# State update in 64 by 64 tiles, last step's stores, and a new order of work in a gated recurrence with a maxout layer

## The chip, the cores and the metric

The kernel runs on one core of one Trainium2 chip. The core has five engines with a queue each: TensorE (PE in the profile, its weight loads PEld), VectorE (DVE), ScalarE (ACT), GpSimd (POOL) and SyncE (SP), which here only issues DMA transfers. The metric is device time in microseconds (us), the median of several runs; lower is better.

## What is computed

Two stages follow each other. The first is a recurrence for 4 batches of 8 heads over 768 tokens, with a state of 48 by 48 per head; the second is a layer that takes the maximum of three products and projects it back.

```python
for t in range(S):
    state = alpha[:, :, t, :, None] * state + np.einsum('bhd,bhe->bhde', k[:, :, t], v[:, :, t])
    y[:, :, t] = np.einsum('bhd,bhde->bhe', q[:, :, t], state)
...
h = np.maximum(np.maximum(x @ w1, x @ w2), x @ w3)
return (h @ w_out).astype(np.float32)
```

x is y with its 8 heads side by side: 3072 tokens of 384 numbers. w1 to w3 are 384 by 768, w_out is 768 by 384.

## The kernel before

The 3072 tokens are worked in 12 steps of 256 tokens (two tiles of 128). Step s belongs to batch s mod 4, so each batch has three steps. In a step the recurrence is turned into matrix products: the logarithms of alpha are summed (`sums`), q and k are scaled by the exponentials of the sums (`scaled`), turned so that the feature dimension lies on the partitions (`turn`, or by a DMA transpose in `turn_by_dma`), multiplied to scores (`scores`), masked (`masked`), and applied to v together with the state left by the earlier tokens (`attend`). `update`, `add_state` and `decay_state` carry the state on. The layer follows: `gate` has nine products a step, `maxed` takes the maximum, `project` multiplies by w_out, `store` scales a tile of 128 tokens and writes it out.

The order of all instructions is written by hand, in three strings: PROLOGUE (the first steps, and the loads of the weights), STEADY (once for each s from 3 to 10) and LAST (s = 11). `emit` reads them piece by piece. A piece is a letter, an index, perhaps a letter for the engine or the memory bank, and the step relative to s after the @: `S0@1` is the state update of step s+1. Each engine executes its own instructions in the order in which the pieces stand, and so does SP with its transfers. The letters:

- l: load of a step (0 alpha, 1 k, 2 q, 3 v); K: load of a weight block (0 to 8 for w1 to w3, 9 to 11 for w_out); W: its cast to fp16
- H: warm matmuls, as many as the index says, on a blank tile; their result is not used
- m, N, r: product of alpha in pairs, logarithms, inverse; u, w: k and q of the first token of a pair; c: sums; e, f, g: their exponentials; k, q: scaling; V: scaling of v
- T, t: turning on TensorE and the copy out of PSUM; D: turning by DMA (from step 5 on); A: scores of one half of the heads; a: mask
- Y: attend; x: its copy; M, S, s, z: gates, update, sum and decay of the state
- G, h: the nine gate products and maxima; O, o: projection and store of one tile

An engine letter is v (VectorE), p (POOL) or a (ACT); without one a default holds: k, q, u, w, m, M, z and W go to POOL, t and s to VectorE, V, x, o and the first h of three to ACT. N, r, e, f and g always run on ACT, the masks and the other h always on VectorE. A letter g behind T, c, A, Y or O (or s) names the PSUM banks; there are four banks g, two s and two w, taken in turn, and a piece that takes a bank waits until the one that had it is read.

The state update (`update`) writes one PSUM tile per tile of tokens x. It contracts over 64 token pairs, so x = 0 lies on partitions 0 to 63 and x = 1 on 64 to 127. The two heads of a pair are 128 columns of weights. In the last four steps, the last of their batch, only x = 0 is updated. The scores (`scores`) use rows of one head (48 of 64) and 64 columns, so four matmuls have tiles of their own.

All loads and stores are issued by SP but the two small constants, which ACT issues at the start. Loads have four buffers per input; a load waits until its buffer has been used.

Of the kernel before, what the change touches and what calls it, by code (L numbers as in the profile page):

```python
# [23 lines left out]
def kernel(  # L24
# [12 lines left out]
    nc = tc.nc  # L37

    B, H, S, D = q.shape
    NT, DM = out.shape  # L40
    DF = moe_w_out.shape[0]
    P = 128
# [3 lines left out]
    U = 2  # L46
    R = 2
# [4 lines left out]
    HP = H // 2  # L52
# [77 lines left out]
    vs_c, ys_c, half_c = c32[:, 0:1], c32[:, 1:2], c32[:, 2:4]  # L130
# [23 lines left out]
    def times(eng, dst, src, col):  # L154
        if eng == "a":
            nc.scalar.mul(dst, src, col)  # L156
        else:
            engines[eng].tensor_scalar_mul(dst, src, col)
# [14 lines left out]
    def bank(shape, name, tag, dtype=FP32):  # L173
        return ps.tile(shape, dtype, name=name, tag=tag, bufs=banks[tag])
# [184 lines left out]
    def update(s, _, tag):  # L359
        qk, vt = qks[s % NQ], vts[s % NQ]  # L360
        xs = range(U) if s + B < NS else range(1)
        for x in xs:
            sps_of[s, x] = bank([P, HP, 2, D], "sps", tag or "s")
        for p in range(HP):
            for r in range(R):
                for x in xs:
                    rows = slice(x * J, (x + 1) * J)
                    nc.tensor.matmul(sps_of[s, x][:, p],  # L368
                                     qk[rows, r, 1, p].rearrange("p a b -> p (a b)"),
                                     vt[rows, r * HP + p, :, :D], start=(r == 0), stop=(r == R - 1))  # L370

    def add_state(s, x, eng):
        c, b = divmod(s, B)
# [48 lines left out]

    def store(s, x, eng):
        c, b = divmod(s, B)
        ob = work.tile([P, DM], FP32, name="ob", tag="ob", bufs=5)
        times(eng or "a", ob, ops_of.pop((s, x)), ys_c)
        row = b * S + (U * c + x) * P
        nc.sync.dma_start(out[row:row + P, :], ob)

    def warm(_, n, *x):  # L430
        wps = bank([P, 512], "wps", "g")
# [8 lines left out]
        "k": scale_k, "q": scale_q, "V": values,  # L440
        "T": turn, "t": keep_turned, "D": turn_by_dma, "A": scores, "a": masked,
        "Y": attend, "x": keep_x, "M": gates, "S": update, "s": add_state, "z": decay_state,
        "G": gate, "h": maxed, "O": project, "o": store,
    }

# [9 lines left out]
    def emit(s, order):  # L455
# [5 lines left out]
                pieces[piece[0]](step, i, eng)  # L461

    PROLOGUE = """
        H7@0 l0@1 l0@2 H4@0 m0p@0 N0@0 H4@0 r0@0 r1@0 H3@0 H1@0 w0p@0
        c0@0 u0v@0 f0@0 H2@0 e0@0 m0p@1 q1v@0 H4@0 V0@0 H6@0 k1v@0 g0@0
        r0@1 N0@1 k0v@0 l2@1 l1@1 l3@1 r1@1 T1@0 q0v@0 l2@2 M0p@0 H3@0
        m0v@2 l1@2 T0g@0 c0g@1 H3@0 N0@2 r0@2 l3@2 t0@0 K2@0 e0@1 g0@1
        S0@0 f0@1 t1@0 K0@0 k1v@1 u0v@1 s0a@0 A0g@0 r1@2 A1g@0 V0@1 l0@3
        c0@2 q1v@1 H5@0 w0p@1 f0@2 a1@0 a2@0 e0@2 k0p@1 g0@2 q0p@1 a3@0
        H4@0 K1@0 T1@1 H2@0 l0@4 M0p@1 t1a@1 z0v@0 s1@0 T0@1 a0@0 K6@0  # L470
        S0@1 u0v@2 Y0g@0 q1p@2 M0p@2 t0a@1 K3@0 w0p@2 s0a@1 k1v@2 V0@2 A1@1
        K7@0 H7@0 K4@0 a3@1 x1@0 a2@1 k0v@2 x0@0 q0p@2 A0g@1 K8@0 z0p@1
        T1@2 a1@1 T0@2 t1a@2 a0@1 Y0g@1 K5@0 t0a@2 W1p@0 A1@2 s1a@1 A0g@2
        W2a@0 W0v@0 S0@2 m0p@3 x1@1 x0v@1 G0@0 s0a@2 G0@1 a2@2 a0@2 a1@2
        l2@3 a3@2 N0@3 r0@4 m0p@4 G1@0 h0@0 l1@3 c0@3 G1@1 r1@4 l3@3
        e0@3 h0v@1 h1@0 W3p@0 G2@1 W6a@0 r0@3 h1@1 f0@3 G2@0 h2@1 G6@0
        z0p@2 h2@0 h6@0 G3@0 W4v@0 h3@0 Y0g@2 K9@0 G4@0 W7p@0 N0@4 r1@3
        x0v@2 c0@4 h4@0 W8p@0 x1@2 G7@0 W5a@0 h7@0 G3@1 h3v@1 K11@0 g0@4
        e0@4 g0@3 w0v@3 G6@1 G8@0 M1p@0 K10@0 h6v@1 G5@0 k1p@3 l2@4 G4@1
        G0@2 l1@4 l3@4 q1p@3 h8@0 h5@0 V0@3 u0p@3 h4@1 G5@1 q0v@3 h5@1  # L480
        G7@1 s1a@2 h0@2 k0p@3 W9a@0 G6@2 f0@4 G8@1 T1@3 h7@1 T0@3 t1a@3
        l1@6 h8@1 W11p@0 h6@2 G1@2 t0@3 l0@5 S0@3 W10p@0 h1@2 A1@3 A0g@3
        z1p@0 k1p@4 a1@3 a0@3 a2@3 a3@3 M0p@3 G3@2 O0g@1 w0v@4 G7@2 s0a@3
        z0p@3 l2@5 o0v@1 O1@0 m0p@5 O0g@0 h7@2 q1v@4 l1@5 s1@3 o1v@0 h3@2
        l3@5 O1g@1 l0@7 r0@5 o1@1 l0@6 G2@2 o0v@0 G4@2 h2@2 l3@6 q0p@4
        h4@2 Y0g@3 l1@7 u0v@4 G8@2 x0v@3 k0p@4 V0@4 l2@6 l3@7 l2@7 x1v@3
        G5@2 h5@2 h8@2 r1@5
    """
    STEADY = """
        T1g@1 u0p@2 T0@1 G0@0 t1@1 N0@2 w0p@2 t0a@1 c0@2 g0@2 h0v@0 f0@2  # L490
        G3@0 q0v@2 G4@0 e0@2 G5@0 G1@0 M1v@-2 h3@0 k1v@2 h4@0 h5@0 z1p@-2
        h1@0 M0p@1 S0@1 q1p@2 k0p@2 D1@2 A0g@1 A1@1 a0@1 V0@2 s0@1 a2@1
        z0p@1 a1@1 G6@0 a3@1 D0@2 s1@1 O1g@-1 O0@-1 h6@0 o1@-1 o0@-1 G7@0
        Y0g@1 G2@0 h7@0 h2@0 r0@3 G8@0 r1@3 x0@1 m0p@3 h8@0 x1@1 l1@5
        l2@5 l0@5 l3@5
    """
    LAST = """
        G0@0 G1@0 G3@0 G6@0 h0@0 G2@0 h1@0 G4@0 h3@0 G7@0 h6@0 G8@0
        h4@0 O1@-1 h2@0 G5@0 h7@0 O0@-1 o1@-1 h8@0 h5@0 o0@-1 O1g@0 O0@0
        o1v@0 o0@0  # L500
    """

    blank = cpool.tile([P, 512], FP16, name="blank")
# [36 lines left out]
```

## Time and profile before

| | |
|---|---|
| median of 5 runs | 155.5 us (155.26 to 156.53) |
| profiled execution | 155.5 us; its span from first to last instruction 153.7 us |
| granted TensorE clock, mean | 0.995 |
| first gate matmul starts | 26.57 us |
| first matmul of STEADY starts | 53.68 us |
| last matmul group starts | 147.04 us |
| matmuls, weight loads | 2539 each |
| bytes moved | 32.50 MB, mean 211 GB/s |

How to read the profile: each engine has a row of its busy time; a group of instructions is named by its line, its engine, and what it writes and reads (gps are the gate products, ops the projection, sps the state update, aps the scores, yps attend, tps the turning, lps the sums, wps the warm matmuls; qk holds scaled q and k, qkT the turned ones, lat the masked scores). Busy time is not time on the path; what sets the end is read from the chain of waits, which goes back from the last instruction to what released it, and from the order of time. The slices by time:

```profile
PE   6997998999999999999999999999999999999990
DVE  2188959979999999699699699696895995784460
DMA  5999999999992899999999999999818047011023
```

Transfers are dense until slice 28 of 40. The steps of STEADY follow each other from about 54 to 139 us, 10.67 us apart.

### The profile page before, as it was taken

Reading aid. Unit: us, or ns where it says so; the run is one execution under the profiler, and the core shown is the slowest. Engines: PE = TensorE matmul, PEld = TensorE weight load, DVE = VectorE, ACT = ScalarE, POOL = GpSimd, SP = SyncE. Lnnn points to the kernel's source line nnn. Section 1 sums busy time; section 2 is a strip of 40 time slices with the busy share of each in tenths; the row PEclk is TensorE's granted clock in tenths of the full one; section 3 lists DMA queues with packets and bytes.
Section 4 is the critical chain, followed back from the end, with each engine's and each line's share of the span. In section 5 each row is a group of like instructions: output and inputs, shape, how many; then the busy total and the mean of one; then the engine's idle time right before and its main releaser. Section 6 shows DMA issues by size and latency. Waiting matters only on the chain.

```text
span 153.7 us, 5939 instructions
## 1 busy us (share of the span) xinstructions
PE 146.8 (96%) x2539; PEld 109.7 (71%) x2539; DVE 119.1 (77%) x214; ACT 82.7 (54%) x164; POOL 82.7 (54%) x112
## 2 busy tenths in 40 slices
PE   6997998999999999999999999999999999999990
PEld 2454656878976797786786886877867877868860
DVE  2188959979999999699699699696895995784460
ACT  3379568984460573753755646646727633143331
POOL 5365977618964259839549469289197280020000
PEclk9999999999999999999999999999999999999998
DMA  5999999999992899999999999999818047011023
GB/s 132 321 325 324 348 335 350 324 256 316 306 289 74 209 339 289 260 142 337 226 198 285 207 271 233 160 294 280 212 40 206 3 63 184 3 51 55 0 75 134
DMA packets 72890, 32.50 MB, mean 211 GB/s; under 512 B 65440, under 2 KB 72864, under 8 KB 72864
## 3 DMA queue, kind: packets, MB, share of 16 engines
q1 hardware_dynamic: 72576, 31.99, 82.5%
q8 instruction: 20, 0.33, 0.9%
q10 hardware_dynamic: 288, 0.13, 0.5%
q14 instruction: 6, 0.05, 0.1%
HBM read 23.73 MB, written 4.72 MB: 185 GB/s over the span
## 4 chain that ended last, share of the span: by engine, by line
PE 77%; DVE 7%; DMA 6%; issue 3%; POOL 2%; ACT 1%; DVEq 0%; POOLq 0%
PE gps L396 36%; PE ops L420 14%; PE wps L433 9%; DMA qkT<-qk 6%; PE yps L330 5%; PE aps L280 4%; PE yps L311 3%; PE sps L368 2%; PE tps L259 2%; DVE hT L411 1%; DVE lat L287 1%; POOL qa L203 1%; DVE qkT L152 1%; DVE qa L203 1%; PE lps L209 1%
## 5 line engine op out<-in xcount | busy, mean ns | idle before, releaser
L396 PE MATMUL gps<-xT,wcat 128*128 128x256 f16 x648 | 77.9, 273 | 0.1
L396 PEld LDWEIGHTS <-wcat 128*128 128x128 f16 x648 | 60.9, 98 | 10.0 <-issue 0.2
L383 POOL TENSOR_TENSOR st<-full,gm 128x384 f16<-128x384 f32 x19 | 17.4, 914 | 31.8 <-DVE gm L355 21.4
L411 DVE TENSOR_TENSOR hT<-gps,h 128x512 f16<-128x512 f32 x36 | 24.2, 689 | 11.9 <-PE gps L396 10.7
L287 DVE TENSOR_TENSOR lat<-aps,cp 128x512 f16<-128x512 f32 x48 | 30.5, 680 | 2.0 <-PE aps L280 1.9
L150 ACT CAST h<-gps 128x512 f16<-128x512 f32 x25 | 14.8, 591 | 27.9 <-PE gps L396 21.9
L411 DVE TENSOR_TENSOR h<-gps,h 128x512 f16<-128x512 f32 x36 | 24.5, 683 | 5.7 <-PE gps L396 3.7
L420 PE MATMUL ops<-wo,hT 128*128 128x384 f16 x144 | 25.4, 326 | 0.0
L156 ACT ACTIVATE ob<-ops,c 128x384 f32<-128x384 f32 x20 | 11.6, 581 | 15.2 <-PE ops L420 15.2
L420 PEld LDWEIGHTS <-hT 128*128 128x128 f16 x144 | 14.1, 98 | 8.0
L433 PE MATMUL wps<-blank 128*128 128x512 f16 x55 | 15.1, 426 | 2.2 <-DVE blank L505 1.2
L184 POOL TENSOR_TENSOR pa<-ra 128x384 f32<-128x384 f32 x11 | 11.1, 1015 | 3.8 <-DMA ra<-in_alpha_dram 3.8
L235 POOL TENSOR_TENSOR qk<-ka,ic 128x384 f16<-128x384 f32 x10 | 10.2, 1018 | 5.4 <-DVE ka L199 4.0
L150 ACT CAST xT<-yps 128x384 f16<-128x384 f32 x20 | 8.7, 483 | 5.7 <-PE yps L330 5.7
L433 PEld LDWEIGHTS <-blank 128*128 128x128 f16 x55 | 5.5, 107 | 8.8 <-issue 3.8
L156 ACT ACTIVATE vt<-rv,c 128x768 f16<-128x768 f32 x12 | 11.5, 956 | 0.5 <-DMA rv<-in_v_dram 0.4
L330 PE MATMUL yps<-lat,vt 64*32 64x128 f16 x768 | 11.1, 220 | 0.5 <-issue 0.2
L203 POOL TENSOR_TENSOR qa<-rq,ra 128x384 f32<-128x384 f32 x10 | 10.0, 1001 | 2.8 <-ACT ra L195 2.3
L330 PEld LDWEIGHTS <-vt 64*32 64x32 f16 x768 | 7.3, 90 | 3.0 <-issue 0.4
L150 ACT COPY qkT<-tps 128x1024 f16<-128x1024 f16 x6 | 5.9, 1014 | 6.2 <-PE tps L259 6.2
L235 POOL TENSOR_TENSOR qk<-rq,ac 128x384 f16<-128x384 f32 x9 | 9.0, 1000 | 0.2 <-issue 0.2
L379 DVE TENSOR_TENSOR full<-sps,st 128x384 f32<-128x384 f32 x16 | 8.7, 546 | 0.0
(52 smaller groups left out, 163.6 us busy)
## 6 DMA issues: line engine op xcount, KB each, us to landing
ra<-in_alpha_dram SPq DMA_DIRECT2D x12, 384.0 KB, 5.5
rk<-in_k_dram SPq DMA_DIRECT2D x12, 384.0 KB, 4.8
rq<-in_q_dram SPq DMA_DIRECT2D x12, 384.0 KB, 5.4
rv<-in_v_dram SPq DMA_DIRECT2D x12, 384.0 KB, 5.6
out_dram<-ob SPq DMA_DIRECT2D x24, 192.0 KB, 3.6
ws<-in_moe_w_dram SPq DMA_DIRECT2D x9, 384.0 KB, 6.0
ws<-in_moe_w_out_dram SPq DMA_DIRECT2D x3, 384.0 KB, 4.8
qkT<-qk SPq DMA_TRANSPOSE x14, 4.8
```

What stands on the lines that cost most here:

```text
L150: nc.scalar.copy(out=dst, in_=src)
L156: nc.scalar.mul(dst, src, col)
L184: engines[eng or "p"].tensor_mul(pair_of[s], raw("a", s, 0), raw("a", s, 1))
L203: engines[eng or "p"].tensor_mul(near_of[s, "q"], raw("q", s, 0), inv1_of.pop(s))
L235: engines[eng or "p"].tensor_mul(dst.rearrange("p a b c -> p (a b) c")[:, :, :D], near_of.pop((s, n)) if r == 0 else raw(n, s, 1), dec_of[ ...
L287: nc.vector.tensor_mul(lat_of[s, u][:, i].rearrange("p (a r) t -> p a r t", r=R), aps_of[s, u][i].rearrange("p (a r) t -> p a r t", r=R), ...
L330: nc.tensor.matmul(yps[x][C * m:C * (m + 1), f, :], vt[rows, r * HP + p].rearrange("p a b -> p (a b)")[:, at:at + C], lats[p // (HP // R)] ...
L383: engines[eng or "p"].tensor_mul(sts[s % B][1 - x].rearrange("p a (b d) -> p a b d", d=D), full_of.pop((s, x)), gm_of.pop((s, x)).unsqueez ...
L396: nc.tensor.matmul(gps[:, j, :], wcat[:, f, g, jj * P:(jj + 1) * P], xT[:, f].rearrange("p u t -> p (u t)"), start=(f == 0), stop=(f == NF ...
L411: nc.vector.tensor_max(h, gps, h_of[s, i - 1])
L420: nc.tensor.matmul(ops, hT_of[s][:, jj, u * P:(u + 1) * P], wo16[:, jj, :], start=(jj == 0), stop=(jj == NJ - 1))
L433: nc.tensor.matmul(wps, blank[:, :P], blank, start=True, stop=True)
```

## The change

`update` splits each matmul in two, one for each head of the pair, with 64 rows and 64 columns. `store` gets a second form: index 2 or 3 stores tile 0 or 1 in two halves of 192 columns, the first scaled by VectorE and issued by SP, the second scaled by ACT and issued on ACT's own queue. LAST uses it as `o2` for tile 0 of the last step. All three order strings are rewritten: pieces stand elsewhere and many run on another engine. The number of pieces other than H is the same; PROLOGUE has 47 warm matmuls in place of 55.

```diff
--- before.py
+++ after.py
@@ -365,9 +365,9 @@
             for r in range(R):
                 for x in xs:
                     rows = slice(x * J, (x + 1) * J)
-                    nc.tensor.matmul(sps_of[s, x][:, p],
-                                     qk[rows, r, 1, p].rearrange("p a b -> p (a b)"),
-                                     vt[rows, r * HP + p, :, :D], start=(r == 0), stop=(r == R - 1))
+                    for i in range(2):
+                        nc.tensor.matmul(sps_of[s, x][64 * i:64 * (i + 1), p], qk[rows, r, 1, p, i],
+                                         vt[rows, r * HP + p, :, :D], start=(r == 0), stop=(r == R - 1))
 
     def add_state(s, x, eng):
         c, b = divmod(s, B)
@@ -422,10 +422,17 @@
 
     def store(s, x, eng):
         c, b = divmod(s, B)
+        split, x = divmod(x, U)
         ob = work.tile([P, DM], FP32, name="ob", tag="ob", bufs=5)
-        times(eng or "a", ob, ops_of.pop((s, x)), ys_c)
         row = b * S + (U * c + x) * P
-        nc.sync.dma_start(out[row:row + P, :], ob)
+        ops = ops_of.pop((s, x))
+        if split:
+            for cols, e, queue in ((slice(0, DM // 2), "v", nc.sync), (slice(DM // 2, DM), "a", nc.scalar)):
+                times(e, ob[:, cols], ops[:, cols], ys_c)
+                queue.dma_start(out[row:row + P, cols], ob[:, cols])
+        else:
+            times(eng or "a", ob, ops, ys_c)
+            nc.sync.dma_start(out[row:row + P, :], ob)
 
     def warm(_, n, *x):
         wps = bank([P, 512], "wps", "g")
@@ -461,43 +468,43 @@
                 pieces[piece[0]](step, i, eng)
 
     PROLOGUE = """
-        H7@0 l0@1 l0@2 H4@0 m0p@0 N0@0 H4@0 r0@0 r1@0 H3@0 H1@0 w0p@0
-        c0@0 u0v@0 f0@0 H2@0 e0@0 m0p@1 q1v@0 H4@0 V0@0 H6@0 k1v@0 g0@0
-        r0@1 N0@1 k0v@0 l2@1 l1@1 l3@1 r1@1 T1@0 q0v@0 l2@2 M0p@0 H3@0
-        m0v@2 l1@2 T0g@0 c0g@1 H3@0 N0@2 r0@2 l3@2 t0@0 K2@0 e0@1 g0@1
-        S0@0 f0@1 t1@0 K0@0 k1v@1 u0v@1 s0a@0 A0g@0 r1@2 A1g@0 V0@1 l0@3
-        c0@2 q1v@1 H5@0 w0p@1 f0@2 a1@0 a2@0 e0@2 k0p@1 g0@2 q0p@1 a3@0
-        H4@0 K1@0 T1@1 H2@0 l0@4 M0p@1 t1a@1 z0v@0 s1@0 T0@1 a0@0 K6@0
-        S0@1 u0v@2 Y0g@0 q1p@2 M0p@2 t0a@1 K3@0 w0p@2 s0a@1 k1v@2 V0@2 A1@1
-        K7@0 H7@0 K4@0 a3@1 x1@0 a2@1 k0v@2 x0@0 q0p@2 A0g@1 K8@0 z0p@1
-        T1@2 a1@1 T0@2 t1a@2 a0@1 Y0g@1 K5@0 t0a@2 W1p@0 A1@2 s1a@1 A0g@2
-        W2a@0 W0v@0 S0@2 m0p@3 x1@1 x0v@1 G0@0 s0a@2 G0@1 a2@2 a0@2 a1@2
-        l2@3 a3@2 N0@3 r0@4 m0p@4 G1@0 h0@0 l1@3 c0@3 G1@1 r1@4 l3@3
...
+        H3@0 H1@0 H8@0 H1@0 m0v@0 r0@0 r1@0 l0@1 N0@0 l1@1 l0@2 c0@0
+        H5@0 H6@0 l2@1 u0p@0 w0v@0 l3@1 H2@0 H2@0 H1@0 m0v@1 l0@3 e0@0
+        H1@0 k1v@0 V0@0 k0p@0 f0@0 l1@2 N0@1 l2@2 q0v@0 c0@1 H2@0 g0@0
+        q1v@0 u0v@1 r0@1 H1@0 r1@1 l0@4 m0p@2 T0g@0 g0@1 t0@0 e0@1 S0@0
+        T1g@0 M0p@0 f0@1 k1v@1 k0p@1 w0p@1 H2@0 t1a@0 H2@0 H2@0 q1v@1 r0@2
+        N0@2 r1@2 K0@0 A0g@0 s0a@0 A1g@0 a0@0 c0@2 V0@1 T1@1 a1@0 H3@0
+        a2@0 q0p@1 m0v@3 K2@0 K1@0 K6@0 f0@2 z0p@0 l2@3 g0@2 t1a@1 a3@0
+        T0g@1 e0@2 H2@0 t0@1 u0v@2 H1@0 N0@3 l3@2 s1a@0 K7@0 M0v@1 A1g@1
+        w0p@2 Y0g@0 x1v@0 q0p@2 c0@3 S0@1 a2@1 K3@0 k0p@2 r0@3 x0@0 s0@1
+        K8@0 W0a@0 T0@2 a3@1 A0g@1 a0@1 H2@0 f0@3 k1p@2 t0a@2 z0p@1 r1@3
+        l1@3 G0@0 q1p@2 a1@1 h0v@0 r0@4 Y0g@1 g0@3 s1a@1 e0@3 W1p@0 K4@0
+        x1@1 m0p@4 T1g@2 x0v@1 W2a@0 K5@0 t1@2 G1@0 G0@1 G2@0 h1@0 l3@3
+        A0@2 W6p@0 h0@1 V0@2 r1@4 w0p@3 G6@0 M0v@2 h2@0 h6@0 l1@4 G1@1
...
+        g0@4 h8@1 W5a@0 k1v@3 k0p@3 G4@1 q0p@3 f0@4 l0@5 Y0@2 h3@1 l2@5
+        M1p@0 G5@1 x1@2 h8@0 x0v@2 h4@1 T1@3 T0g@3 e0@4 t1@3 h5@1 z1p@0
+        G5@0 G4@0 t0a@3 G0@2 l3@6 h4@0 G6@2 V0@3 u0p@4 h6@2 h5@0 S0@3
+        A0@3 W10a@0 A1g@3 h0v@2 W11p@0 a2@3 G1@2 s0a@3 z0p@3 G7@2 l1@6 l3@4
+        W9a@0 a3@3 w0p@4 G8@2 l1@5 h7@2 G3@2 s1a@3 O1@1 q1p@4 a1@3 h1@2
+        o1@1 q0p@4 O1@0 O0@0 h8@2 l0@6 a0@3 o0v@0 m0p@5 l2@6 k0v@4 k1v@4
+        l3@5 h3@2 O0g@1 o1@0 Y0g@3 G4@2 o0v@1 G2@2 V0v@4 x0@3 x1@3 l1@7
+        l2@7 G5@2 l3@7 l0@7 h4@2 h2@2 r0@5 r1@5 h5@2
     """
     STEADY = """
-        T1g@1 u0p@2 T0@1 G0@0 t1@1 N0@2 w0p@2 t0a@1 c0@2 g0@2 h0v@0 f0@2
-        G3@0 q0v@2 G4@0 e0@2 G5@0 G1@0 M1v@-2 h3@0 k1v@2 h4@0 h5@0 z1p@-2
-        h1@0 M0p@1 S0@1 q1p@2 k0p@2 D1@2 A0g@1 A1@1 a0@1 V0@2 s0@1 a2@1
-        z0p@1 a1@1 G6@0 a3@1 D0@2 s1@1 O1g@-1 O0@-1 h6@0 o1@-1 o0@-1 G7@0
-        Y0g@1 G2@0 h7@0 h2@0 r0@3 G8@0 r1@3 x0@1 m0p@3 h8@0 x1@1 l1@5
-        l2@5 l0@5 l3@5
+        T1g@1 T0@1 M0p@1 u0v@2 N0@2 G0@0 c0@2 t1@1 w0v@2 t0a@1 G3@0 G4@0
+        h3v@0 G1@0 h0@0 r0@3 g0@2 G5@0 M1p@-2 h4@0 r1@3 z1p@-2 f0@2 e0@2
+        h1@0 h5@0 V0@2 k0p@2 S0@1 s0@1 z0p@1 A0g@1 a0@1 A1@1 k1p@2 G7@0
+        O1@-1 a3@1 G6@0 q0p@2 s1@1 q1p@2 a1@1 a2@1 D0@2 D1@2 l3@5 l1@5
+        l2@5 O0g@-1 h6v@0 o1@-1 l0@5 o0@-1 h7@0 Y0@1 x0@1 x1@1 G8@0 G2@0
+        h8@0 m0p@3 h2@0
     """
     LAST = """
-        G0@0 G1@0 G3@0 G6@0 h0@0 G2@0 h1@0 G4@0 h3@0 G7@0 h6@0 G8@0
-        h4@0 O1@-1 h2@0 G5@0 h7@0 O0@-1 o1@-1 h8@0 h5@0 o0@-1 O1g@0 O0@0
-        o1v@0 o0@0
+        G0@0 h0v@0 G6@0 G1@0 G3@0 G4@0 h3@0 h1@0 O0@-1 h4@0 h6@0 G2@0
+        h2@0 G5@0 h5@0 o0v@-1 G7@0 G8@0 O1@-1 h7@0 o1@-1 h8@0 O0@0 o2v@0
+        O1@0 o1@0
     """
 
     blank = cpool.tile([P, 512], FP16, name="blank")
```

## The prediction

> **What bounds the kernel now.** First the busy row of TensorE and its slices, then its waits, then the chain of waits, then the order of time at both ends.
>
> ```profile
> PE 146.8 (96%) x2539; PEld 109.7 (71%) x2539; DVE 119.1 (77%) x214; ACT 82.7 (54%) x164; POOL 82.7 (54%) x112
> PEclk9999999999999999999999999999999999999998
> ```
>
> The waits, longest in total (us, times, longest), and the group of the warm matmuls:
>
> ```profile
> PE wps L433 <- DVE lat L287: 1.0, 1, 1.0
> PE aps L280 <- DMA qkT<-qk: 0.3, 1, 0.3
> L433 PE MATMUL wps<-blank 128*128 128x512 f16 x55 | 15.1, 426 | 2.2 <-DVE blank L505 1.2 <-DVE lat L287 1.0
> ```
>
> One step in the view by windows (TensorE, its loads, VectorE, ACT, POOL busy, clock, transfers):
>
> ```profile
> 75.00:85.67 10.67, 10.67 (x210) 8.30 (x209) 9.08 (x17) 6.22 (x13) 7.11 (x10) 1.00 1.11 230
> ```
>
> TensorE is the bound. The reader is to see that it has nearly no wait: of the 153.7 us span it is idle 6.9. The window row is one steady step: TensorE busy 10.67 of 10.67, VectorE 9.08, and the transfers share is over 1, so SP's queue is full as well. The time can fall in three ways only: fewer wasted matmuls and waits at the front (55 warm matmuls, 15.1 us, all before 23 us), a cheaper step, or a shorter tail after the last matmul.
>
> **Part 1, the state update in 64 by 64 tiles.** The view in order of time around one update (start, duration, ...):
>
> ```profile
> 90.56 0.51 PE L368 MATMUL sps<-vt,qk 64*128 64x96 f16 x16
> 91.00 0.64 PE L280 MATMUL aps<-qkT 48*64 48x128 f16 x32
> 91.58 0.61 PE L396 MATMUL gps<-xT,wcat 128*128 128x256 f16 x4
> ```
>
> And the two groups of weight loads (busy, mean ns):
>
> ```profile
> L280 PEld LDWEIGHTS <-qkT 48*64 48x64 f16 x384 | 5.8, 106 | 2.2 <-DMA qkT<-qk 0.7 <-DVE qkT L152 0.5 <-issue 0.4
> L368 PEld LDWEIGHTS <-qk 64*128 64x128 f16 x160 | 4.4, 94 | 2.5 <-issue 2.3
> ```
>
> An update is 16 matmuls, two side by side (x = 0 and 1): 8 rounds of 96 columns, 0.44 us from its start to the start of the scores. The scores are 8 rounds of four tiles of 128 columns, 0.58 us. The transposes (the chain has 16 of 128 columns, all in the full array, in 0.89) give 56 ns for a round of 128 columns, so 42 ns for 96. Thus 8 x 42 = 0.34 of the update's 0.44 and 8 x 56 = 0.45 of the scores' 0.58 is streaming. The rest, 0.10 and 0.13, sits where the tile shape changes. The same is at the next border: in the chain the six gate matmuls after the scores take 0.76, others 0.66. After the change an update is 32 matmuls, four side by side, still 8 rounds of 96 columns; and where scores follow it directly, the shape no longer changes between them. That removes about 0.11. They follow directly in the eight steps of STEADY and at steps 2 and 3: ten times, **1.0 to 1.1 us**, all on TensorE's path.
>
> Against it speaks a rule. The Trainium skill, TensorEngine Tiling (Array Packing), Restrictions, says that column tiling switches off the fast weight load; TensorE: Matmul & The Clock Gate, LDWEIGHTS, gives a load P/1.2 ns. For 64 columns that is 53 ns, over the 42 of a round: 8 x 11 = 0.09 more per update, 12 updates, 1.1 us: the whole gain eaten. The rows: a load of 64 columns takes 106 ns, one of 128 columns in the update 94, only 12 more, and the scores keep to 56 ns a round with 64-column loads. That shows a load at most 56 and does not show 42. I take the rows, no loss, because 12 ns more on a load that runs beside the round before it is little, and keep the rule's end: part 1 lies between -1.3 and +0.1, I take **-1.0**. On the mode change itself the same page's Key Properties (a change of mode drains the array) agrees with 0.10 to 0.13 here.
>
> **Part 2, the front.** The whole order is rewritten, and this is the larger edit: 47 warm matmuls for 55, loads, engines and order moved. The first ten warm matmuls take 0.43 each (cold), later ones 0.218 (12 in 2.61). Eight fewer warm ones are worth 1.7 us only if no wait takes their place, so I walk the new order with the rows' durations. A 128x384 operation costs 0.47 on VectorE, 0.95 on POOL, 0.45 on ACT; a mask 0.61, a copy of 1024 0.61 on VectorE and 0.9 on ACT; results are seen 0.1 to 0.2 later. Loads: POOL ends its wait for alpha of step 0 at 4.62 and for K1, 15 loads later in SP's order, at 23.75, so load n lands near 4.62 + 1.27n.
>
> ```profile
> 4.62 0.99 POOL L184 TENSOR_TENSOR pa<-ra 128x384 f32<-128x384 f32 x1 [1.98 <-DMA ra<-in_alpha_dram]
> 7.42 0.33 PE L209 MATMUL lps<-la,cp 128*128 128x384 f16 x1
> 13.36 0.64 PE L280 MATMUL aps<-qkT 48*64 48x128 f16 x32
> 23.75 0.82 POOL L152 CAST wcat<-ws 128x768 f16<-128x768 f32 x1 [1.71 <-DMA ws<-in_moe_w_dram]
> 26.57 2.14 PE L396 MATMUL gps<-xT,wcat 128*128 128x256 f16 x18
> ```
>
> Before, c0@0 runs at 7.42, behind 19 warm ones; A@0 at 13.36; G0@0 at 26.57. After: 13 warm ones end at 6.1, c0@0 at 6.3 (m0 on VectorE halves its 0.99). V0@0 now stands ahead of f0@0 on ACT and waits for v, so q0 is scaled at 11.0. c0@1 10.7, T0@0 11.6, S0@0 12.1, T1@0 12.5; six warm ones; A@0 14.25, c0@2 15.0, T1@1 15.25. T0g@1 waits for POOL's q0 to 17.0; A1g@1 for ACT's t1 to 18.6; Y@0, c0@3, S0@1 to 20.6. Then T0@2 waits for POOL: q of step 2 is load 11, 18.6; w0, q0, k0 one after the other, 21.5 to 22.0, a wait of 0.9 to 1.4. A0g@1 needs banks that a2 and a3 free, 22.5; G0@0 at **23.2** (W0 is load 13, 21.1, cast by 22.1). Y@1 waits for the masks to 24.2. From there each gate finds its weights: W1 25.8 for 25.8, W6 27.6 for 28, W7 (load 19, 28.8) 29.6 for 31, W3 30.9 for 31.7.
>
> At its first gate before had already done what after does later: Y@1 1.1, T1@2 0.45, half the scores of 2 0.57, S0@2 0.45, less c0@3 0.25: 2.3 us. After at 24.2 has G0 done, before at 27.2; 24.2 + 2.3 = 26.5: **0.7 to 1.0 us** earlier, I take 0.8. Ends: if q comes a load earlier and no port is shared, 1.4; if VectorE and POOL hold each other up twice more, as where an operation took 1.36 instead of 0.55 on VectorE at 9.80, -0.6 (a loss). A wait of 1.0 (the warm matmuls on a mask) left the clock row full; one of 1.4 no row shows, and I count no slower clock for it.
>
> **Part 3, the steady order.** TensorE's work per step is the same but for part 1; each other engine must keep up. VectorE trades q0, k1 and a gate pair for u0, w0 and one more of the h group: u0, w0 1.0, eight h 4.9, s 0.95, masks 2.4: about 9.2 of 10.56. Tightest is a2@1: s1 now stands before a1 and a2, so the masks end 7.7 to 7.8 us after the step's G0, and Y uses them at 8.1. Before is as tight: in the trace the last mask ends 7.8 after G0. POOL: its chain k0, z0, k1, q0, q1, m0 starts at e0 (3.3) and ends at 9.6; N0 needs m0 by about 10.6. D0 and D1 now wait for q0 and q1 (7.7, 8.6), where before the second left SP at 9.15 behind loads; SP has D ahead of the four loads and two stores, about 10.4 us of transfers in a step. A pair takes 4 to 5 us, lands near 13, and the scores ask at 14.5. All fits, at slacks of 0.4 to 1.5. The two waits before (scores on qkT, 0.3 and 0.2) may go; I cost the steady order at **0**, ends -0.4 and +3.
>
> **Part 4, the tail.**
>
> ```profile
> 148.82 2.28 SPq L428 DMA_DIRECT2D out_dram<-ob  x3
> 149.19 0.62 DVE L158 TENSOR_SCALAR ob<-ops,c 128x384 f32<-128x384 f32 x1 [1.26 <-PE ops L420]
> 150.17 0.58 ACT L156 ACTIVATE ob<-ops,c 128x384 f32<-128x384 f32 x1 [1.37 <-PE ops L420]
> ```
>
> The split does not fall on the tile that ends last: o2 is tile 0, and O1, o1 (whole, ACT, SP) follow it. Before the end is 0.58 on ACT and 2.9 of store after the last matmul; after it is the same: **0**. ACT's half and its store's issue (0.4, as ACT's two issues at the start) fit into the 0.98 of O1's matmuls; without that cover, +0.4. LAST keeps 9 gates and 4 projections in both.
>
> **Sum** against the profiled execution (155.5, span 153.7 and 1.8 around it, equal to the median of 155.5): -1.0 - 0.8 + 0 + 0 = -1.8, **153.7**.
>
> **Rivals.** *Loads slow the new tiles*: by the rule above part 1 is +0.1: 154.8. For it: no row shows four loads within 42 ns. *The front returns nothing*, each removed warm matmul becomes a wait: 154.5. For it: T0@2, A0g@1 and Y@1 all wait in my walk. *Slower: VectorE at Y*. If s0 to a2 end later than walked, Y waits every step and everything behind it. It decides from 0.4 lateness, and against the gain from 0.4 + 1.8/8 = 0.63; at 0.8 it costs 0.4 x 8 = 3.2, thus 156.9. For it: VectorE at nine tenths and one more operation ahead of the masks. Against it: the masks follow each other at 0.61 in the rows, and u0, w0 run when POOL hardly reads. *The split does nothing* holds in all cases.
>
> **Chances.** Forecast 0.57 (own range 152.6 to 154.6), slow loads 0.13, empty front 0.10, slower 0.20. A difference under 0.5% (0.78 us) can't be told from none. Faster takes nearly all of the forecast, some of the two middle ones: 0.66; same 0.15; slower 0.19. Range 152.5 to 156.4.
>
> **What would show it.** Update to scores: no gap, scores 0.47 instead of 0.58; loads at 42 ns a round or 53. First gate near 23, STEADY's first matmul about 0.8 to 1 earlier than 53.7. In STEADY no row of Y waiting on masks, and none of the scores on qkT. The last scaling 0.58 on ACT, as before. I am wrong if the steps do not shrink to 10.56, or a wait in the front exceeds 1.5.

## The result, and the profile after

| | before | after |
|---|---|---|
| median, us | 155.94 (80 runs) | 156.25 (43 runs) |
| ratio of times, 95% interval | | 0.9985 [0.9968, 1.0003] |
| profiled execution: span, us | 153.7 | 153.5 |
| first gate matmul starts | 26.57 | 23.02 |
| first matmul of STEADY starts | 53.68 | 54.48 |
| last group of 18 projection matmuls starts | 147.04 | 146.45 |
| last scaling starts | 150.17 | 149.98 |

There is no change that can be told from none. (The ratio leaves disturbed executions out, the medians contain them.) The profiled executions say where the time went. From the first instruction to STEADY the new kernel is 0.80 **later**; from there to the last projection group it is 1.39 **faster** (91.97 for 93.36); from that group to the last scaling it is 0.40 **slower** (3.53 for 3.13). The sum, -0.19, is how much earlier the last scaling starts; the spans differ by 0.2.

The steady part first. The order of time of TensorE in one step after (start, duration, what, count):

```profile
80.12 0.54 PE L369 MATMUL sps<-vt,qk 64*64 64x96 f16 x32
80.49 0.62 PE L280 MATMUL aps<-qkT 48*64 48x128 f16 x32
81.04 0.83 PE L396 MATMUL gps<-xT,wcat 128*128 128x256 f16 x6
```

The update takes 0.37 to the start of the scores (0.44 before), the scores 0.55 to the start of the gates (0.58 before), together 0.92 (1.02 before). The group of the update's weight loads (count, busy, mean ns):

```profile
L369 PEld LDWEIGHTS <-qk 64*64 64x64 f16 x320 | 4.8, 106 | 2.2 <-issue 2.1
```

A load is now recorded at 106 ns, where it was 94; the update is shorter all the same. Next, the waits of TensorE over the whole span, in us: total, times, longest:

```profile
PE yps L330 <- issue: 1.4, 1, 1.4
PE wps L440 <- DVE blank L512: 1.2, 1, 1.2
PE tps L259 <- POOL qk L235: 0.9, 2, 0.6
PE lps L209 <- ACT la L188: 0.5, 1, 0.5
PE aps L280 <- DVE qkT L152: 0.3, 1, 0.3
```

In this execution the scores wait for no turned tile by DMA any more, and the largest wait is a new one: 1.4 us of attend, for nothing that the profile shows ("issue"). The order of time of TensorE around it, and the first group of STEADY:

```profile
23.02 0.82 PE L396 MATMUL gps<-xT,wcat 128*128 128x256 f16 x6
...
23.94 0.49 PE L330 MATMUL yps<-lat,vt 64*32 64x128 f16 x29
25.87 0.34 PE L330 MATMUL yps<-lat,vt 64*32 64x128 f16 x19 [1.44 <-issue]
...
27.06 2.13 PE L396 MATMUL gps<-xT,wcat 128*128 128x256 f16 x18
...
54.48 0.72 PE L259 MATMUL tps<-cp,qk 128*128 128x128 f16 x10
```

The 48 matmuls of one attend group are cut after the 29th. Their data are there: the other 19 read the same tiles. From 27.06 on TensorE has no wait row up to STEADY (one gap of 0.30, explained below, is too short for a row), so what is lost up to there is not made up. The tail, in the order of time of all engines:

```profile
146.45 3.09 PE L420 MATMUL ops<-wo,hT 128*128 128x384 f16 x18
...
148.61 0.42 DVE L158 TENSOR_SCALAR ob<-ops,c 128x192 f32<-128x192 f32 x1 [0.66 <-PE ops L420]
...
149.06 0.42 ACT L156 ACTIVATE ob<-ops,c 128x192 f32<-128x192 f32 x1 [0.84 <-DVE ob L158]
149.51 0.37 ACTq L432 DMA_DIRECT2D out_dram<-ob  x1
149.98 0.58 ACT L156 ACTIVATE ob<-ops,c 128x384 f32<-128x384 f32 x1 [0.50 <-PE ops L420]
```

The two halves do not run beside each other: ACT's half waits for VectorE's half (both write one tile, `ob`, and read one tile, `ops`; the row does not say which of them binds), then ACT issues its store, and only then scales the tile that ends last.

### The profile page after: what moved, and what is told of

It is laid out like the page before. It is cut to its first block, busy times and chain, and to the rows that moved or that the text cites. A ratio compares the mean times of both kernels' runs of the same rounds, so it can differ in the third digit from the quotient of the medians.

```text
span 153.5 us, 6225 instructions
## 1 busy us (share of the span) xinstructions
PE 145.0 (94%) x2691; PEld 108.3 (71%) x2691; DVE 120.5 (79%) x212; ACT 77.7 (51%) x156; POOL 84.8 (55%) x123
## 4 chain that ended last, share of the span: by engine, by line
PE 84%; DVE 3%; DMA 3%; SPq 2%; issue 2%; POOL 1%; ACT 1%; ACTq 0%; POOLq 0%
PE gps L396 48%; PE ops L420 15%; PE yps L330 6%; PE aps L280 4%; PE yps L311 4%; PE sps L369 3%; DMA ra<-in_alpha_dram 3%; PE tps L259 2%; SPq L95 2%; PE wps L440 2%; POOL qk L235 1%; DVE lat L287 1%; PE lps L209 1%; DVE pa L184 1%; ACT ob L156 1%
## 5 line engine op out<-in xcount | busy, mean ns | idle before, releaser
L156 ACT ACTIVATE ob<-ops,c 128x384 f32<-128x384 f32 (+1 forms) x21 | 12.1, 574 | 38.4 <-PE ops L420 37.5
L420 PE MATMUL ops<-wo,hT 128*128 128x384 f16 x144 | 26.5, 326 | 0.0
L353 POOL TENSOR_TENSOR gt<-ge 128x4 f32<-128x4 f32 x17 | 4.2, 250 | 21.6 <-ACT ge L229 21.6
L150 ACT CAST h<-gps 128x512 f16<-128x512 f32 x16 | 9.3, 586 | 10.4 <-PE gps L396 7.2
L152 DVE CAST h<-gps 128x512 f16<-128x512 f32 x20 | 13.7, 685 | 1.0 <-PE gps L396 0.9
L440 PE MATMUL wps<-blank 128*128 128x512 f16 x47 | 13.2, 426 | 1.2 <-DVE blank L512 1.2
L235 POOL TENSOR_TENSOR qk<-ka,ic 128x384 f16<-128x384 f32 x11 | 11.4, 1033 | 0.3 <-ACT ic L217 0.2
L235 POOL TENSOR_TENSOR qk<-qa,ac 128x384 f16<-128x384 f32 x11 | 11.0, 999 | 0.2
L156 ACT ACTIVATE vt<-rv,c 128x768 f16<-128x768 f32 x11 | 10.3, 938 | 1.3 <-DMA rv<-in_v_dram 1.3
L184 POOL TENSOR_TENSOR pa<-ra 128x384 f32<-128x384 f32 x9 | 9.0, 1003 | 3.5 <-DVE ka L199 3.5
```

Of the source, the lines that this page charges most:

```text
L150: nc.scalar.copy(out=dst, in_=src)
L152: engines[eng].tensor_copy(out=dst, in_=src)
L184: engines[eng or "p"].tensor_mul(pair_of[s], raw("a", s, 0), raw("a", s, 1))
L235: engines[eng or "p"].tensor_mul(dst.rearrange("p a b c -> p (a b) c")[:, :, :D], near_of.pop((s, n)) if r == 0 else raw(n, s, 1), dec_of[ ...
L420: nc.tensor.matmul(ops, hT_of[s][:, jj, u * P:(u + 1) * P], wo16[:, jj, :], start=(jj == 0), stop=(jj == NJ - 1))
L440: nc.tensor.matmul(wps, blank[:, :P], blank, start=True, stop=True)
```

## What the unexplained wait is

The instructions of TensorE reach it in blocks: the page lists q8, kind "instruction", with 21 packets (20 before) of 16,384 bytes. TensorE has 5,399 records in the trace (5,092 before): 5,382 matmuls and weight loads (5,078 before), the others its sequencer's. That is about 256 to a packet, so I take a block as 256 records. I counted them, from 0 and in the order of their starts, and set the start of each block packet beside them. In before and in after, and in every variant that has a gap in this attend group, it lies exactly ahead of record 705, whichever matmul that is (the 30th of 48 in after, the second of 16 in before, the sixth of 16 in experiments 10 and 11); so it is not something that one matmul reads. Other gaps of this kind lie a multiple of 256 further on: at 961 in experiment 1 (3.32), at 1473 in after (0.30), at 3009 in experiment 11 (0.46). In the front the packet that brings the block of record 705 starts only after record 449 has started, which is when the block before the last is used up. Where TensorE stood and waited, it went on 2.2 to 2.7 us after the packet's start. From the traces (us; a gap is counted here from the start of the record before it, so it is 0.2 to 0.3 more than the idle time in the rows; the last columns are the edits of the variants below):

```
kernel                         record 449  packet  later by  gap at 705  STEADY  masks of 2,3  update of 0,1
before                           20.10     22.91     2.81      0.46      53.68   (old order)   64x128
after                            19.42     23.46     4.04      1.65      54.48   VectorE       64x64
after_whole_tile                 19.38     23.77     4.39      1.82      54.5    VectorE       64x64
after_old_tiles_steps01          19.85     22.84     3.00      0.09      54.57   VectorE       64x128
after_steps01_whole_tile         19.94     23.50     3.56      0.88      54.3    VectorE       64x128
after_masks_on_pool              19.30     23.48     4.18      1.40      54.6    GpSimd        64x64
few_weight_loads                 19.41     23.35     3.94      1.44      54.4    GpSimd        64x64
steps01_masks_on_pool            19.90     23.94     4.04      1.18      54.3    GpSimd        64x128
steps01_masks_whole_tile         19.74     23.14     3.40      0.67      53.5    GpSimd        64x128
front_weights_alone              19.22     23.20     3.98      0.68      54.1    GpSimd        64x64
front_without_loads              19.27     20.67     1.39      0.00      53.5    GpSimd        64x64
```

The working theory that the experiments test: **the block is late, because its packet waits behind the data loads**, and small tiles use 256 instructions up sooner. An update of two tiles in 64 by 64 has 32 records more.

## The experiments

Each ratio is against the kernel before, run on the same chip beside it.

### 1. The new tiles in the old order

```diff
--- before
-                    nc.tensor.matmul(sps_of[s, x][:, p], qk[rows, r, 1, p] ...
+                    for i in range(2):
+                        nc.tensor.matmul(sps_of[s, x][64 * i:64 * (i + 1), p], qk[rows, r, 1, p, i], ...
```

> The kernel before with the update in 64 by 64 tiles and nothing else. Theory T (the saved change of tile shape is real and lies on TensorE's path): scores right after an update take 0.45 us instead of 0.57 in the chain, a STEADY step 10.56 instead of 10.67, ten such places, so about 1.0 us less than before, ratio near 0.993. Rival (slow loads of 64 columns, or TensorE's gain caught by another engine): step stays 10.67, ratio 1.00. Theory F (TensorE ran out of instructions at its record 705, because they come in blocks of 256 by DMA behind the loads): there are 64 more instructions ahead of that point, so a wait without a releaser stands again at record 705, now 64 instructions earlier in the program, between 0 and 0.5 us.

Ratio **1.0313** [1.0266, 1.0360]: the new tiles alone, in the old order, cost about 4.9 us (3.13% of 155.9). The waits of TensorE, in part:

```profile
PE gps L396 <- issue: 3.1, 1, 3.1
PE aps L280 <- DMA qkT<-qk: 1.4, 3, 0.7
...
PE yps L330 <- issue: 1.1, 1, 1.1
```

There are two block waits: at record 705 (1.35) and 256 records on, at 961 (3.32; its packet started 4.07 after record 705). And in the steady part the faster step runs into DMA-turned tiles that come no sooner. The clock row of the page:

```profile
PEclk9999999959999999999999999999999999999999
```

In the slice in which the wait of 3 us ends the granted clock falls to half. The waits of 1.0 to 1.4 us in before and after left no mark in their clock rows.

### 2. The new order with the old tiles

The reverse edit, on the kernel after.

> The changed kernel with the update in two tiles of 64 by 128 as before, the new order and the split kept. Theory T: steps of 10.67 again, about 1.0 to 1.1 us slower than the changed kernel, 0.8 slower than before, ratio near 1.005. Theory F: the wait without a releaser stands at record 705 again, which is 64 instructions later in the program (behind the first 48 matmuls of the attend group of step 1, not behind its 29th), still above 1 us. Rival to F (the wait belongs to what the 30th matmul reads or writes): it stays in front of the same matmul.

Ratio 1.0008 [0.9984, 1.0031]. Steps are 10.67 again, so the 0.11 a step is the tiles'. The gap at 705 shrank to 0.25, where I had expected more: with two updates in old tiles, record 705 lies 64 instructions later in the work, and the block has the more time. The expected size was a miss. STEADY starts at 54.6 all the same, behind waits for GpSimd's q and k (1.7 in all) and for a mask of VectorE (0.7).

### 3. The last tile whole

```diff
--- after (LAST)
-        h2@0 G5@0 h5@0 o0v@-1 G7@0 G8@0 O1@-1 h7@0 o1@-1 h8@0 O0@0 o2v@0
+        h2@0 G5@0 h5@0 o0v@-1 G7@0 G8@0 O1@-1 h7@0 o1@-1 h8@0 O0@0 o0v@0
```

> The changed kernel with tile 0 of the last step scaled whole by VectorE and stored by SP, in place of the two halves. Theory: the ACT half waits for the VectorE half, and ACT then issues a store before it can scale the last tile, which starts 0.4 us late; so about 0.35 us less than the changed kernel, last scaling at 149.6 in place of 149.98 if the rest is equal, ratio to before near 0.996. Rival (the tail hides it): no difference, ratio 0.9985.

Ratio **0.9954** [0.9928, 0.9980]. The tail in its trace:

```profile
147.80 3.09 PE L420 MATMUL ops<-wo,hT 128*128 128x384 f16 x18
...
149.95 0.62 DVE L158 TENSOR_SCALAR ob<-ops,c 128x384 f32<-128x384 f32 x1 [0.65 <-PE ops L420]
150.97 0.58 ACT L156 ACTIVATE ob<-ops,c 128x384 f32<-128x384 f32 x1 [1.42 <-PE ops L420]
```

From the last projection group to the last scaling it is 3.17 (after 3.53): the split costs 0.36 us. The projection group itself starts later here than in after (146.45), and that has nothing to do with the tail. This execution has a wait in the steady part that the same order of work did not have in after:

```profile
PE aps L280 <- DMA qkT<-qk: 1.0, 1, 1.0
```

So the new order does not keep the turned tiles in time in every execution.

### 4. Attend later

```diff
--- after (PROLOGUE)
-        l1@3 G0@0 q1p@2 a1@1 h0v@0 r0@4 Y0g@1 g0@3 s1a@1 e0@3 W1p@0 K4@0
-        x1@1 m0p@4 T1g@2 x0v@1 W2a@0 K5@0 t1@2 G1@0 G0@1 G2@0 h1@0 l3@3
+        l1@3 G0@0 q1p@2 a1@1 h0v@0 r0@4 W1p@0 T1g@2 G1@0 Y0g@1 g0@3 s1a@1
+        e0@3 K4@0 t1@2 x1@1 m0p@4 x0v@1 W2a@0 K5@0 G0@1 G2@0 h1@0 l3@3
```

> The changed kernel with the attend group of step 1 moved behind the turning of step 2 and the second gate product (with the cast of its weights and the copy of the turned tile moved along). Theory F: the block of instructions arrives near 25.9 while TensorE waits for POOL and does gates, so the wait without a releaser falls to below 0.3 us and the first matmul of STEADY starts 0.4 to 0.6 us earlier than in the changed kernel; ratio near 0.995. Rival (the wait belongs to the attend group): it moves along with it and stays 1.4, ratio 0.9985 or worse.

Ratio 1.0041 [1.0015, 1.0067]. The gap at 705 is gone, as the block theory has it; the time is a miss. The order of time of TensorE shows what took its place:

```profile
24.96 0.62 PE L259 MATMUL tps<-cp,qk 128*128 128x128 f16 x8 [0.74 <-POOL qk L235]
...
28.49 0.72 PE L396 MATMUL gps<-xT,wcat 128*128 128x256 f16 x5 [0.69 <-DVE xT L152]
```

The work moved ahead was not ready, and the gates wait for an attend that is now late. A gap of 0.68 stands at record 1473, and STEADY starts at 55.7.

### 5 and 6. Old tiles in steps 0 and 1 alone, and the same with the last tile whole

```diff
--- after (update)
+                    if s < 2:
+                        nc.tensor.matmul(sps_of[s, x][:, p], qk[rows, r, 1, p] ...
+                    else:
                     for i in range(2):
...
```

> The changed kernel with the old tiles for the updates of steps 0 and 1 only (where no scores follow them), new tiles from step 2 on. Theory F (blocks of 256 instructions, each fetched by DMA only when the block two before it is used up): 64 fewer instructions ahead of record 705, so the wait there falls from 1.65 to 0.3 or so, as in the run with old tiles everywhere, while the steps stay 10.56; about 1 us less than the changed kernel, ratio near 0.992. Rival (the front is bound by POOL and the loads, and a shorter wait there is lost to the next): ratio 0.9985 again, STEADY's first matmul at 54.4 as in the changed kernel.

> The run before this one with the last step's tile 0 whole on VectorE. The two gains are at different ends, so they add: 0.35 to 0.5 us below the run with old tiles in steps 0 and 1, ratio near 0.989.

Ratios 0.9986 [0.9964, 1.0009] and **0.9950** [0.9928, 0.9972]. The tail's gain adds; the front's does not come. In the first the gap was 0.09, and STEADY still starts at 54.57. What is late next, in the order of time of TensorE:

```profile
30.89 0.81 PE L401 MATMUL gps<-xT,wcat 128*128 128x256 f16 x6 [0.21 <-DVE hT L416]
...
32.96 0.41 PE L280 MATMUL aps<-qkT 48*64 48x128 f16 x15 [0.75 <-DVE lat L287]
```

and, of the same kernel, VectorE and then GpSimd in order of time:

```profile
27.59 1.79 DVE L353 TENSOR_TENSOR gt<-ge 128x4 f32<-128x4 f32 x1
29.41 0.82 DVE L355 TENSOR_TENSOR gm<-gt,c 128x8 f32<-128x8 f32 x1
```

```profile
27.59 1.01 POOL L203 TENSOR_TENSOR qa<-rq,ra 128x384 f32<-128x384 f32 x1
28.53 1.69 POOL L152 CAST wcat<-ws 128x768 f16<-128x768 f32 x2
```

Two tiny VectorE operations of the gates' masks (`M0v@2`; 4 and 8 numbers a partition) take 1.79 and 0.82. The first ends at 29.38, half way through GpSimd's pair of casts, the second at 30.23, where the pair ends (30.22). In after the same two take 0.15 and 0.17, at a time when GpSimd waits for the load of a weight block (VectorE, then GpSimd):

```profile
28.53 0.15 DVE L353 TENSOR_TENSOR gt<-ge 128x4 f32<-128x4 f32 x1
28.71 0.17 DVE L355 TENSOR_TENSOR gm<-gt,c 128x8 f32<-128x8 f32 x1
```

```profile
27.11 1.01 POOL L203 TENSOR_TENSOR qa<-rq,ra 128x384 f32<-128x384 f32 x1
29.23 0.82 POOL L152 CAST wcat<-ws 128x768 f16<-128x768 f32 x1 [1.11 <-DMA ws<-in_moe_w_dram]
```

The Trainium skill (SBUF — State Buffer, two separate sides) has a rule for this: a VectorE operation with two SBUF inputs and a GpSimd operation that reads SBUF share a pair of ports, which one of them holds for its whole instruction. The second of the two operations agrees with it; the first was held through two of GpSimd's operations, 27.59 to 29.36. So behind the block stands a second bound, and the block wait hid it.

Its size varies. Where old tiles in steps 0 and 1 made the block wait shorter (experiments 2, 5 and 6), the scores wait 0.7, 0.75 and 0.3 for a mask. Part of the gain was gone before that: attend of step 1 starts at 24.45, 24.35 and 24.17 in these three, where it was 23.77 in after, behind longer waits for GpSimd's q and k. For experiment 5 the parts add up: 0.58 later at attend, 1.56 less at record 705, 0.96 more in the two rows above. So the smaller gap is not the tiles' work alone: the packet started 0.62 sooner than in after, and TensorE came to record 705 later for that earlier wait as well. Why GpSimd was later in these kernels was not looked into.

### 7. The old front with the new steady part

The PROLOGUE of before (loads l1@5, l1@6 and l3@5 each moved ahead, as the new STEADY asks), old tiles up to step 3, STEADY and LAST of after, last tile whole.

> PROLOGUE of the kernel before (with the loads of k and v of step 5 moved ahead of those of step 6, which STEADY needs first), STEADY and LAST of the changed kernel with the whole tile, old tiles up to step 3 and new ones from step 4. Theory (front lost, steady order and tiles won): the first matmul of STEADY near 53.7, steps of 10.56 without waits on the turned tiles, span near 152.4, ratio near 0.990. Rival (the new steady order lives on the new front's loads being ahead): waits in the first steps, ratio 0.996 or above.

Ratio 1.0008 [0.9973, 1.0042]. STEADY starts at 53.65, but its first step takes 11.5 us, with this wait in it:

```profile
59.69 0.41 PE L280 MATMUL aps<-qkT 48*64 48x128 f16 x15 [0.71 <-ACT ic L217]
```

The later steps are 10.56. The row names ACT's operation `ic`, and ACT was late because it had waited 1.56 for an alpha load, up to 57.80. In this arrangement the new steady order still pays in its first step for loads that the old front has not brought ahead.

### 8. The new tiles in the old steady order, from step 4 on

The condition is `s < 4` for the old tiles, on the kernel before, so the front is untouched.

> The kernel before with the new tiles from step 4 on only, so that its front has the same instructions as before. Theory: the step wants 10.56, but in the old order the turned tiles leave SP late, and the scores wait for them as soon as TensorE is faster: more than half of the 0.9 us is given back in waits of the scores on DMA, ratio 0.996 to 0.999. Rival (the old order can follow): steps of 10.56 and ratio 0.993.

Ratio 1.0027 [1.0004, 1.0050]. One line of the waits says where:

```profile
PE aps L280 <- DMA qkT<-qk: 1.2, 2, 0.8
```

Eight steps should save 0.11 each, 0.9; but 0.9 more than before's 0.3 is waited for turned tiles, and two single steps take 11.52 and 11.19. From the first update of STEADY to its last, seven steps, this trace needs 75.7, before 74.9 and after 73.7. In the old order the update's gain is paid back, and in this execution more than that. With the new order of STEADY no profile but that of experiment 3 has such a wait.

### 9 to 11. The masks on GpSimd

```diff
--- after (PROLOGUE)
-        A0@2 W6p@0 h0@1 V0@2 r1@4 w0p@3 G6@0 M0v@2 h2@0 h6@0 l1@4 G1@1
-        a0@2 G2@1 K10@0 M0v@3 h1@1 G6@1 a1@2 S0@2 W7p@0 h2@1 W8a@0 W3p@0
+        A0@2 W6p@0 h0@1 V0@2 r1@4 w0p@3 G6@0 h2@0 h6@0 l1@4 G1@1
+        a0@2 G2@1 K10@0 h1@1 G6@1 a1@2 S0@2 W7p@0 h2@1 W8a@0 W3p@0
...
-        G8@1 G3@1 h3v@0 q1p@3 z0p@2 l2@4 h7@1 G8@0 c0@4 s1a@2 W4a@0 u0p@3
+        G8@1 G3@1 h3v@0 M0p@2 M0p@3 q1p@3 z0p@2 l2@4 h7@1 G8@0 c0@4 s1a@2 W4a@0 u0p@3
```

Alone, then with old tiles in steps 0 and 1, then with the last tile whole as well:

> The changed kernel with one edit: the gates' masks of steps 2 and 3 (two VectorE operations each, L353 and L355) go to GpSimd, just before q1 of step 3. The 64x64 update stays everywhere. Theory (two bounds in series in the front: the missing instruction block before Y of step 1 at TensorE's record 705, and behind it VectorE's mask operations[...]): the first bound is still there, so the front gains at most 0.3 us: ratio 0.996 to 1.001, with an idle stretch that has no releaser at record 705. Rival (the mask operations alone are the bound): STEADY's first matmul at 53.8 or earlier and a ratio near 0.993.

> The old 64x128 tiles in the updates of steps 0 and 1 alone, so that the instruction block of record 705 is in time, and the masks of steps 2 and 3 on GpSimd; the last tile still in halves. Theory (two bounds in series): both bounds are away, STEADY's first matmul comes at 53.5 to 53.9 instead of 54.5, and the ratio is 0.991 to 0.995 (0.6 to 1.0 us below the same kernel with the masks on VectorE, 0.9986). Rival (a third bound stands behind these two, the weights' casts on GpSimd or the turned rows of step 2): STEADY's first matmul stays at 54.2 to 54.6 and the ratio at 0.997 to 1.0.

> The kernel before this one, with output tile 0 stored whole by VectorE. Theory: the tail's 0.35 to 0.5 us comes on top: ratio 0.987 to 0.992, the best of all. Rival (a third bound in the front): 0.993 to 0.997, no better than the same kernel with the masks on VectorE (0.995).

Ratios 0.9992 [0.9963, 1.0022], 0.9957 [0.9934, 0.9981] and **0.9937** [0.9909, 0.9966]. The first is as expected: the block bound is still there (gap 1.40). The second and the third fall short of the forecast, because old tiles in two steps do not keep the block in time in every execution: their profiles have gaps of 1.18 and 0.67. The table agrees with two bounds: in the new order with the masks on VectorE, STEADY starts at 54.3 to 54.6 whatever the gap is, 0.09 to 1.82; with them on GpSimd a smaller gap goes with an earlier start in these three (1.40, 1.18, 0.67 give 54.6, 54.3, 53.5). The relation is loose: 1.44 gives 54.4 in experiment 12, 0.68 gives 54.1 in experiment 14. The third is the fastest of all kernels that keep every load, 1.0 us below before, but its interval overlaps those of the two other kernels with a whole tile, and the second's overlaps that of the same kernel with the masks on VectorE (0.9986). With the gap down to 0.67 and the masks moved, STEADY starts 0.2 before that of the old kernel, not the 0.8 of the forecast.

### 12. Fewer weight loads

On the kernel of experiment 9, `load_weight` returns at once for blocks 3 to 8, and the casts read `stage[i % 3]`, so the results are others than the reference's.

> The changed kernel with the masks of steps 2 and 3 on GpSimd, and six of the nine loads of the first layer's weights left out (the casts read the three blocks that are loaded, so the gates' weights are not the reference's; loads of 2.3 MB less between 17 and 30 us). The 64x64 update stays everywhere, and no instruction of TensorE is changed, so record 705 is the same one. Theory (the instruction block waits behind the data loads on the same DMA engines): its fetch starts at most 2 us after record 449 instead of 4.2, the idle stretch at record 705 is under 0.3 us instead of 1.2 to 1.7, and STEADY's first matmul comes at 53.3 or earlier instead of 54.5; ratio 0.985 to 0.993. Rival (the fetch takes its 6 us whatever the data loads do): a stretch of over 1 us at record 705, and STEADY's first matmul after 54.

A miss: gap 1.44, packet 3.94 late, ratio 0.9957 [0.9932, 0.9983]. The traffic was not thinned: SP's queue runs in order, so input loads moved up into the empty places, and the transfers' share stays at 0.98 to 1.14 in every stretch from 18 to 32 us. It does show that the arrival of blocks 3 to 8 of the weights is not what holds STEADY at 54.4.

### 13 and 14. The front without input loads, with few and with all weight loads

```diff
--- experiments 12 and 9
     def load(n, s):
+        if s >= 2:
+            return
...
-        return rings[n][s % NQ][:, :, r]
+        return rings[n][s % 2][:, :, r]
```

(and the same in `values`; every step uses the inputs of step 0 or 1.)

> The changed kernel with the masks of steps 2 and 3 on GpSimd, six of nine weight loads left out, and the loads of q, k, v and alpha of step 2 and later left out too (every step reads the inputs of step 0 or 1, so the output is another; 5 MB less in the front). TensorE's instructions stay the same. After 17 us the DMA engines have little to do. Theory (the instruction block waits behind the data loads): the block's packet starts at most 1.6 us after record 449 instead of 3.9 to 4.2, and the idle stretch before record 705 is under 0.3 us. Rival (the fetch's 4 us belong to the fetch itself): the packet starts 3 us or more after record 449, and the stretch is 1 us or more where TensorE gets through 256 records in under 5.5 us.

> The same with all weight loads left in: only the inputs of step 2 and later are not loaded. Between 17 and 24 us the weights' nine loads (3.5 MB) fill the DMA engines alone, sooner than before, since no input load stands between them. Theory: the delay lies with the bytes in flight at the time of record 449: 2 to 4 us if the loads are still under way at 19.5 us, under 1.6 us if they are through. Rival (the fetch's own 4 us): 3 us or more in both kernels.

There is one execution of each, 154.45 and 155.13 us, beside 155.79 for before; single times differ by more than that, so only the traces are read. The transfers between record 449 and 23 us, first without loads, then with the weights' loads in flight (rows of the DMA view: busy tenths in 40 slices, and the packets of the instruction queue or of the data):

```profile
DMA  0000000000000060000000000000000000000000
...
q8 instruction: 1, 0.02, 1.6%
```

```profile
DMA  9999999999999999999999999999999999989989
...
q1 hardware_dynamic: 1254, 1.32, 110.4%
```

With the engines empty the packet of the block starts 1.39 after record 449, and there is no gap; with weight loads under way it starts 3.98 after, and TensorE stands at the same record. The row of the second kernel:

```profile
25.82 0.34 PE L332 MATMUL yps<-lat,vt 64*32 64x128 f16 x19 [0.47 <-issue]
```

The instructions of TensorE are the same, and up to that attend the two kernels are within 0.05 us of each other (24.55 and 24.50; both reach it 0.5 later than experiment 9, for waits of their own). STEADY starts at 53.5 and 54.1: a gap of 0.68 costs 0.6. The trace without loads has both cases in itself: at record 193, while the first loads still fill the engines, the packet starts 2.61 late; from record 705 to 1729, with the engines nearly empty, 0.61 to 1.00 late. That the block comes late because of the data loads in flight is **shown**, by one execution of each kernel. Some delay, 0.6 to 1.4, stays without them.

## Why the prediction was wrong

The prediction was 153.7, 1.8 below the kernel before; measured is no difference. By its parts:

- **Part 1, the update, -1.0: right in size.** Update and scores together save 0.10 to 0.11 a step, 0.9 in eight steps; the two places in the front can't be measured apart. The sign "scores 0.47 instead of 0.58" did not come: of the 0.10, 0.07 came off the update (0.44 to 0.37) and 0.03 off the scores (0.55). A round takes at most 46 ns (0.37 / 8, with what is left at the border), under the 53 that the prediction had worked out from the rule for loads, so the rival "loads slow the new tiles" falls, although each load is recorded 12 ns longer. What the prediction did not say: in the old order the gain is given back in waits for turned tiles (experiments 1 and 8).
- **Part 3, the steady order, 0: a little better than that**, at its own end of -0.4. Steps are 10.56, and the two waits on qkT went (in this profile; experiment 3 had one of 1.05). With part 1 that makes the 1.39 between STEADY's start and the last projections. The rival of a late VectorE did not come.
- **Part 4, the tail, 0: measured +0.40, of which the split is 0.36 (experiment 3).** The step that failed is "ACT's half and its store's issue fit into the 0.98 of O1's matmuls". They do not, for ACT's half starts 0.42 late, behind VectorE's half. The prediction named the price without cover, 0.4, and took the cover for granted.
- **Part 2, the front, -0.8: measured +0.80, wrong by 1.6; here the forecast failed.** The walk itself held: first gate 23.02 (23.2 forecast), A@0 14.35 (14.25), T1@1 15.32 (15.25), A1g@1 18.53 (18.6), T0@2 21.90 (21.5 to 22.0). The step that failed is the next one: "Y@1 waits for the masks to 24.2. From there each gate finds its weights". Attend started at 23.77, and the gates did find their weights; attend did not find its own **instructions**, and stood for 1.44 at record 705. The walk put this at nothing: it has TensorE wait for data and banks only. On paper, without this wait and the 0.3 at record 1473, 54.48 becomes 52.7, the forecast's "0.8 to 1 earlier than 53.7". No run reached that; the earliest start of STEADY is 53.5.
- Where the block was in time, other waits took the gain: GpSimd's q and k ahead of attend, and the masks of step 2 on VectorE while GpSimd works without a pause (experiment 5, gap 0.09, STEADY at 54.57). The prediction had this in its range ("if VectorE and POOL hold each other up twice more"), but not at this place. The rival "the front returns nothing" was nearest for the front (it lost 0.8), for a reason that it did not name.

The profile of before had the sign, inside an attend group that had begun, with all data there:

```profile
24.86 0.23 PE L330 MATMUL yps<-lat,vt 64*32 64x128 f16 x1
25.32 0.30 PE L330 MATMUL yps<-lat,vt 64*32 64x128 f16 x15 [0.23 <-issue]
```

That is the same record 705, with a gap of 0.46. The new order reached record 449 0.7 sooner and used the 256 instructions from there in 4.8 us, as before, while the packet started 0.5 later. So the whole lead, and more, was lost.

Open: a profile is one execution. Kernels with equal instructions on TensorE had gaps between 0.09 and 1.18 (experiments 5, 6, 10, 11), and three with the front of before had 0.46, 0.00 and 0.64 (before, experiments 7 and 8), so the share of the gap in a median is known only roughly. Of the ACT half's wait I have the row and its cost; whether the shared `ob` or the shared `ops` makes it wait was not tried. What keeps the front from the forecast's 52.7 to 52.9 once both bounds are smaller was not found, nor why a fetch with little traffic still starts 0.6 to 1.4 us late.

## What to carry to other kernels

An idle stretch without a releaser, in the middle of a group whose data are there, can be a missing block of instructions: count the engine's instructions between such places, and where transfers are dense, price a front not by its arithmetic alone but also by how fast it uses its instructions up. Cutting a matmul into more, smaller ones raises that count, so it pays in a steady part and can cost in a front that is full of loads. Where a wait goes, look for the next bound behind it before its gain is booked, and where two engines are meant to work on two halves at the same time, check in the trace that the second does not start after the first (whether two tiles in place of one would free it here was not tried).

## What was not expected of the hardware

- TensorE's instructions come in blocks of 256. Counted from the record that uses up the block before the last, the packet for the next started 2.2 to 4.8 us after it at record 449 in the dense front, and in the steady part from 3.2 after to 2.2 before it; where it waited, TensorE went on 2.2 to 2.7 after the packet's start. The Trainium skill (Runtime: NRT & Kernel Launch, Instruction fetch mechanics) has the block size, and says that crossing a border is mostly hidden; here it cost 1.44 in after and 3.05 in experiment 1. The same section gives TensorE room for 2048 instructions and, in a note, only two lines; Advanced Engine Details and Errata (ISA Cache) also has only two lines, of 256 each. The traces agree with the two.
- A wait of 3.05 ended in a slice at half the granted clock (experiment 1); waits of 1.0 to 1.4 did not.
- Two VectorE operations of 0.15 and 0.17 took 1.79 and 0.82 beside GpSimd (after against experiment 5).
